# Second-layer trunk sums kept in PSUM over a chunk, four of its products by two levels, on one Trainium2 core

## The chip, the cores and the metric

The kernel runs on one core of a Trainium2 chip. The metric is the device time of one execution, in microseconds; lower is better. The engines are named as in the profile: TensorE (PE, with its weight loads as PEld) multiplies matrices, VectorE (DVE) and ScalarE (ACT) do elementwise work, GpSimd (POOL) does elementwise work and issues some DMAs, and SyncE (SP) issues most DMAs. SBUF is the on-chip memory, PSUM the eight accumulator banks that TensorE writes (each 128 partitions by 512 fp32 numbers).

## The reference

A retention block (a decayed linear attention) feeds a two-layer network with a leaky ReLU. Everything is fp32 in the result.

```python
# q, k, v: batch 4, 8 heads, 768 tokens, 64 dims
gamma = 1.0 - 2.0 ** (-5.0 - np.arange(H))
for t in range(S):
    state = gamma[None, :, None, None] * state + np.einsum('bhd,bhe->bhde', k[:, :, t], v[:, :, t])
    y[:, :, t] = scale * np.einsum('bhd,bhde->bhe', q[:, :, t], state)
x = y.transpose(0, 2, 1, 3).reshape(B * S, H * D)      # 3072 x 512
h = x @ w_in                                           # 512 -> 2048
g = np.maximum(0.01 * h, h)
return g @ w_out                                       # 2048 -> 512
```

## The kernel before

**Tiling.** The 768 tokens of each of the four sequences are cut into six chunks of 128, so a chunk c has 512 tokens in all. The 2048 hidden columns are cut into four units u of 512. For each pair (c, u) the kernel computes a hidden block (first layer), applies the leaky ReLU, and adds that unit's part to the output of the chunk (second layer). All matrix products of a pair are made by Strassen-Winograd: a 512x512x512 product is cut into 2x2 blocks of 256, and seven block products M1 to M7 replace eight. Their operands are blocks (b11, ...) and sums and differences of blocks, made on VectorE or GpSimd; their results are combined in PSUM and on VectorE.

**Two halves.** The first half (to about 285 us) covers chunks 0 and 1 and turns the weights from 64-bit to fp32. It also stores to DRAM the sums of first-layer weights ("kept") that the second half streams back. The second half runs over n = 0 to 15, n = 4(c-2) + u, in a loop at the end of the kernel. In this half the first layer is made by two levels of Strassen-Winograd: `inner_steps(n, group)` runs the second level for four of the seven products (group 0, weights `wa`, 28 matmuls of 128x128) or the other three (group 1, weights `wb`, 21 matmuls of 128x128), in banks 0 to 3, and `outer(n, group)` combines them on VectorE into g. The list INNER gives the order of the seven second-level products: M1, M5, M4, M6, M2, M3, M7. ScalarE copies M1's bank to the bank of M6 and M7, and takes four of the results out; VectorE adds the rest (L611 `plus`, L614 `minus`: nearly all VectorE additions have these two lines in the profile, so they are told apart by their tiles).

**The second layer.** For n = 0 to 3 and n = 15, `output` makes seven products of one level (28 matmuls of 128x256) in banks 5, 4, 7, 6 (called A, B, C, D), and each is added to the chunk's output tile o. For n = 4 to 14 (`by_leaves`), two ways are mixed. `trunk` makes four products by one level, M1 into A, M5 into C, M6 and M7 into B (16 matmuls of 128x256, L1299); A is copied to B after M1, B is added to o after M6 and again after M7, and `trunk_taken` adds A and C. The other three products (the "leaves") are made by the second level: `leaf_steps` (21 matmuls of 128x128, L1261, banks 6, 7, 2, 5), with weights that `sums_of_rows` made on VectorE in n = 0 to 3 and stored to DRAM (`leaf_kept`), and that `load_rows` reads back for every n. The moving operands are four differences on GpSimd (`leaf_sums`, L1252). The results stand in a tile and are added to o by an accumulating DMA issued from GpSimd (L1283), or on VectorE at the last unit of a chunk.

**Attention inside the loop.** While chunk c is in the network, the attention of chunk c+1 is made in pairs of sequences, at u = 0 and u = 1 (`visiting`, n = 0, 1, 4, 5, 8, 9). `joint_visit` makes the outputs of a pair in banks 1, 2, 0 and 7, and four VectorE instructions (L468) write them to x. `scores_of_pair` makes the scores (banks 0, 1) and state sums (banks 2, 3) of the pair that is visited next; VectorE masks the scores and adds the states. There are scores in n = 0, 1, 4, 5 and 8. `differences` and `sums_of_x` make the Strassen-Winograd operands of x.

**Order.** The order of the instructions on each engine is the order in which the program writes them; each engine runs its own queue in order. In a unit with leaves TensorE runs: first-layer group 0 of n+1; the visit; trunk M1, M5, M6; the scores; trunk M7; group 1 of n+1; the leaf. Where there are no scores, trunk M7 stands behind group 1. Units without a visit skip the attention parts. A DMA on SyncE's queue that waits holds up those behind it.

Of the kernel before, what the change touches and what calls it, by code (L numbers as in the profile page):

```python
# [18 lines left out]
C = 128  # L19
# [3 lines left out]
def kernel(  # L23
# [334 lines left out]
    def scores_of_pair(c, b, banks=None, mid=None):  # L358
# [28 lines left out]
        for j in range(2):  # L387
            am = work.tile([128, 2, HP // 2, 2, C // 2], FP32, tag=f"am{j}", name=f"am{j}_{c}_{b}")
            nc.vector.tensor_tensor(
                out=am.rearrange("p b m i t -> p (b m i) t"),  # L390
                in0=at[j].rearrange("p b m i t -> p (b m i) t"),
                in1=mask[:, 0].unsqueeze(1).to_broadcast([128, 2 * HP, C // 2]), op=ALU.mult)
            weights.append(am)
# [7 lines left out]
        if not last:  # L401
            state_of[p] = halves_of_states.pop(0)
            plus(state_of[p], mid, sums[1])
        mid_of[p] = old, mid
# [9 lines left out]
    def joint_visit(c, b, banks=None):  # L414

        later = following(c, b) if c > JOINED else None
        banks = banks or [[bank[k] for k in at] for at in ((1, 2), (0, 7))]
# [193 lines left out]
    def plus(out, a, b):  # L611
        nc.vector.tensor_tensor(out=out, in0=a, in1=b, op=ALU.add)  # L612

    def minus(out, a, b):  # L614
        nc.vector.tensor_tensor(out=out, in0=a, in1=b, op=ALU.subtract)  # L615
# [13 lines left out]
    def differences(x, t, last=True):  # L629

        minus(t[:, 0], x[:, 1], x[:, 0])
        minus(t[:, 1], x[:, 3], t[:, 0])
        minus(t[:, 2], x[:, 2], t[:, 1])
        if last:
            last_difference(x)

    def last_difference(x):
        minus(x[:, 1], x[:, 3], x[:, 1])
# [169 lines left out]
    last_three = {}  # L808
# [9 lines left out]
    def new_g(c, u):  # L818
        i = slot[0]
        slot[0] = 1 - i  # L820
        both = work.tile([128, 7, 2, N], FP32, tag=f"g{i}", name=f"g_{c}_{u}")
        last_three[c, u] = both[:, 2:5]
        return u, both[:, 0:4], Reversed(both)
# [309 lines left out]
    def sums_of_x(c, group):  # L1133
# [3 lines left out]
        for blocks, made in (((x[:, 0:1], made[:, :, 0:1]), (t, made[:, :, 1:4])) if group == 0 else  # L1137
# [5 lines left out]
            minus(b12, b22, b12)  # L1143
# [40 lines left out]
    leaf_kept = [dram.tile([128, 3, 7, C], FP32, name=f"leaf_kept_{u}") for u in range(NU)]  # L1184
# [3 lines left out]

    def leaf_rooms():

        free = [flat_of(unit(k)[:, 2:5]) for k in (1, 3, 5)]
        spare = [x2_place[0][:, 21 * C :], streamed_flat[0][:, 21 * C :]]
        more = [spare[i // 2][:, ds(i % 2 * 3 * C, 3 * C)] for i in range(4)]
        return free, spare, [x.rearrange("p (q n) -> p q n", q=3) for x in more]

    def rows_of(u):

        if u < NU - 1:
            return [((0, 3, 1), unit(2 * u + 1)[:, 2:5])]
        return [((0, 3, 2), units[2 * u + 1][1]), ((1, 2, 1), last_s4)]  # L1200

    def sums_of_rows(u):

        free, _, more = leaf_rooms()
        if u == NU - 1:
            more = more[0:2] + [x[:, 7 * C : 10 * C].rearrange("p (q n) -> p q n", q=3)
                                for x in free[0:2]]
        bases = []
        for at, blocks in rows_of(u):
            which = slice(*at)  # L1210
            a11, a21, a12, a22 = (blocks[:, :, k, ts(m, C)] for k in range(2) for m in range(2))
            r = [x[:, which] for x in more]
            plus(r[0], a21, a22)
            minus(r[1], r[0], a11)
            minus(r[2], a12, r[1])
            minus(r[3], a11, a21)
            bases.append((which, blocks))

        def keep():
            for which, blocks in bases:  # L1220
# [4 lines left out]
            for j, r in enumerate(more):  # L1225
                nc.sync.dma_start(out=leaf_kept[u][:, :, 3 + j], in_=r)
        return keep

    def load_rows(n):

        free, spare, _ = leaf_rooms()
        leaf_weights[:] = [x[:, 0 : 7 * C].rearrange("p (j n) -> p j n", j=7)
                           for x in (free[0], free[1], spare[1])]
        for to, kept_rows in zip(leaf_weights, (leaf_kept[at_of(n)[1]][:, i] for i in range(3))):
            nc.sync.dma_start(out=to, in_=kept_rows)

    leaf_weights = []

    def by_leaves(n):
        return n >= NU and n < N2 - 1  # L1240

    def leaf_sums(n):

        free, spare, _ = leaf_rooms()
        made = [x.rearrange("p (q n) -> p q n", q=3)
                for x in (free[0][:, 7 * C : 10 * C], free[1][:, 7 * C : 10 * C],
                          spare[0][:, 0 : 3 * C])]
        three = last_three[at_of(n)]
        b11, b12, b21, b22 = (three[:, :, k, ts(h, C)] for k in range(2) for h in range(2))
        for out, a, b in ((made[0], b12, b11), (made[1], b22, made[0]), (made[2], b21, made[1]),  # L1250
                          (b12, b22, b12)):
            nc.gpsimd.tensor_tensor(out=out, in0=a, in1=b, op=ALU.subtract)  # L1252
        return [b11, b21, *made, b22, b12]

    def leaf_steps(n, moving):

        ps = [bank[i][:, 0 : 3 * C].rearrange("p (i n) -> p i n", i=3) for i in (6, 7, 2, 5)]
        results = leaf_results()
        for m, q, j, s in INNER:
            for i in range(3):  # L1260
                nc.tensor.matmul(ps[q][:, i], lhsT=leaf_weights[i][:, j], rhs=moving[s][:, i],  # L1261
# [6 lines left out]
            elif m == "M7":  # L1268
                plus(results[:, :, 3], results[:, :, 3], ps[3])
                plus(results[:, :, 2], results[:, :, 2], ps[3])  # L1270
# [5 lines left out]
    def leaf_results():  # L1276
        return flat_of(unit(5)[:, 2:5]).rearrange("p (i q n) -> p i q n", i=3, q=4)

    def leaf_results_taken(c, o, final):

        results = leaf_results()
        if not final:
            nc.gpsimd.dma_start(out=o[:, 0:3].rearrange("p i k n -> p (i k n)"),  # L1283
                                in_=results.rearrange("p i q n -> p (i q n)"), accum_op=ALU.add)
            return
        for i in range(3):
            plus(o[:, i], o[:, i], results[:, i].rearrange("p (k h) n -> p k (h n)", k=2))
            nc.sync.dma_start(out=out[c, i], in_=o[:, i])

    def trunk(c, o, part, first, final):  # L1290

        u, g, gd = part
        ps = {x: room[x] for x in "ABC"}
        for m, x, sa, rhs, start in (("M1", "A", 0, g[:, 0], True), ("M5", "C", 4, gd[:, 0], True),
                                     ("M6", "B", 5, gd[:, 1], False),
                                     ("M7", "B", 1, g[:, 1], False)):
            for i in range(2):
                for k in range(2):
                    nc.tensor.matmul(ps[x][:, i, :], lhsT=block(2 * u + 1, sa)[:, k, ts(i, 128)],  # L1299
                                     rhs=rhs[:, k, :], start=(start and i == 0 and k == 0),  # L1300
                                     stop=(k == 1), skip_group_check=True)
            if m == "M1":
                nc.scalar.copy(out=ps["B"], in_=ps["A"])  # L1303
            elif m == "M6":
                if first:
                    nc.scalar.copy(out=o[:, 1], in_=ps["B"])
                else:
                    plus(o[:, 1], o[:, 1], ps["B"])
            elif m == "M7":
# [301 lines left out]
```

## Time and profile before

| | us |
|---|---|
| three runs | 634.63, 634.06, 633.66 (median 634.06) |
| the profiled execution, device time | 633.81 |
| its span in the profile | 632.1 |
| VectorE busy | 498.1 |
| ScalarE busy | 283.5 |
| GpSimd busy | 81.4 |
| DMA, mean over the span | 223 GB/s |
| granted TensorE clock | 1.00 |

A profile row reads: line, engine, operation, output tile <- input tiles, shape and count. One fp32 matmul of the program appears as two MATMUL records with two weight loads. In a timeline the first number is the start in microseconds from the start of the span and the second the time from the first start to the last end of the merged instructions; matmuls overlap their successors by some 0.16 us, so times between starts say what one costs. What stands in brackets is idle time and what ended it.

Start times of the units in the second half, taken from the first matmul of group 0 of n+1: n=1 before 285.9, n=2 at 304.98, n=3 at 328.01, n=4 at 351.04, n=5 at 378.02, n=6 at 405.08, n=7 at 427.62, n=8 at 450.16, n=9 at 477.16, n=10 at 502.88, n=11 at 525.42, n=12 at 547.97, n=13 at 570.84, n=14 at 593.38. The output of n=15 starts at 615.92, the last matmul at about 628.5.

### The profile page before, as it was taken

The page shows a single profiled execution, that of the slowest core. Times are in us where ns is not written, and L with a number is a line of the kernel's source. Part 1 is how long each engine was busy: PE and PEld are TensorE (multiplying, and loading weights), DVE is VectorE, ACT ScalarE, POOL GpSimd, SP SyncE. Part 2 cuts the span into 40 slices and gives each one's busy share as a digit, 9 for nine tenths or more (in the row PEclk, how much of TensorE's full clock was granted, in tenths as well). Part 3 has the DMA queues.
Part 4 walks back from the last instruction along what each step waited for, and adds up shares of the span by engine and source line. Part 5 has one row for each costly group of instructions (what it writes and reads, how often), then busy time and mean ns, then how long its engine had stood idle before and what let it go on. Part 6 is the DMA issues. An engine that isn't in the chain of part 4 may idle for free.

```text
span 632.1 us, 15063 instructions
## 1 busy us (share of the span) xinstructions
PE 624.7 (99%) x6284; PEld 570.5 (90%) x6284; DVE 498.1 (79%) x803; ACT 283.5 (45%) x559; POOL 81.4 (13%) x98
## 2 busy tenths in 40 slices
PE   8999999999999999999999999999999999999997
PEld 5888888888888889899999999999998999999996
DVE  5679769889979976668887768799848889866765
ACT  5876646347443114352442452634434424544540
POOL 2000000000011010101000033313033023033200
PEclk9999999999999999999999999999999999999999
DMA  8941325547772998295964888998479579689724
GB/s 330 404 138 34 133 67 208 163 145 226 260 276 81 334 350 289 89 347 168 340 209 157 280 293 250 342 293 260 157 240 306 159 230 278 206 263 271 192 45 116
DMA packets 103219, 141.18 MB, mean 223 GB/s; under 512 B 4328, under 2 KB 82024, under 8 KB 103152
## 3 DMA queue, kind: packets, MB, share of 16 engines
q1 hardware_dynamic: 101552, 132.53, 63.3%
q0 software_dynamic: 1296, 7.08, 5.6%
q8 instruction: 49, 0.80, 0.5%
q10 hardware_dynamic: 304, 0.62, 0.3%
q14 instruction: 18, 0.15, 0.1%
HBM read 108.49 MB, written 24.64 MB: 211 GB/s over the span
## 4 chain that ended last, share of the span: by engine, by line
PE 90%; DMA 5%; ACT 2%; DVE 2%; issue 0%; SPq 0%; DVEq 0%; ACTq 0%
PE bank L1348 26%; PE bank L1299 12%; PE bank L668 11%; PE bank L1261 8%; PE C_h L668 4%; PE B_o L668 4%; PE A_h L668 4%; PE A_o L668 4%; PE C_o L668 4%; PE B_h L668 4%; PE D_o L668 2%; PE D_h L668 2%; DMA x_words<-in_weights_dram 1%; DMA wa<-kept 1%; DMA in<-in_kv_dram 1%; PE bank L371 1%
## 5 line engine op out<-in xcount | busy, mean ns | idle before, releaser
L612 DVE TENSOR_TENSOR made<-made,bank 128x512 f32<-128x512 f32 (+1 forms) x96 | 56.1, 617 | 39.9 <-PE bank L1348 35.9
L1348 PEld LDWEIGHTS bank<-x,wb 128*128 128x128 f32 x672 | 77.6, 192 | 1.1 <-ACT bank L1352 0.3
L1348 PE MATMUL bank<-x,wb 128*128 128x128 f32 x672 | 77.9, 275 | 0.1
L612 DVE TENSOR_TENSOR o<-o,bank 128x512 f32<-128x512 f32 (+3 forms) x75 | 55.2, 767 | 24.3 <-ACT bank L782 6.2
L615 DVE TENSOR_TENSOR g<-g 128x512 f32<-128x512 f32 x96 | 64.1, 688 | 5.3 <-ACT g L1390 0.6
L1348 PE MATMUL bank<-x,wa 128*128 128x128 f32 x512 | 67.6, 275 | 0.0
L1299 PE MATMUL bank<-g,w 128*128 128x256 f32 x288 | 66.1, 382 | 0.7 <-DVE x L468 0.7
L1348 PEld LDWEIGHTS bank<-x,wa 128*128 128x128 f32 x512 | 62.8, 192 | 0.3
L1299 PEld LDWEIGHTS bank<-g,w 128*128 128x128 f32 x288 | 53.2, 190 | 8.0 <-DVE x L468 1.1
L1348 PE MATMUL bank<-t,wa 128*128 128x128 f32 x384 | 53.4, 275 | 0.1
L1348 PEld LDWEIGHTS bank<-t,wa 128*128 128x128 f32 x384 | 48.0, 192 | 0.3 <-DMA wa<-kept 0.3
L612 DVE TENSOR_TENSOR g<-made 128x512 f32<-128x512 f32 x64 | 44.0, 709 | 3.0
L1352 ACT COPY bank<-bank 128x512 f32<-128x512 f32 (+1 forms) x32 | 16.6, 520 | 60.1 <-PE bank L1348 59.8
L1390 ACT ACTIVATE g<-g 128x512 f32<-128x512 f32 x64 | 38.5, 631 | 8.2 <-DVE g L612 8.2
L668 PE MATMUL bank<-g,w 128*128 128x256 f32 x168 | 38.0, 382 | 0.0
L668 PEld LDWEIGHTS bank<-g,w 128*128 128x128 f32 x168 | 31.3, 190 | 4.2
L668 PE MATMUL bank<-g,last 128*128 128x256 f32 (+1 forms) x148 | 32.6, 375 | 0.0
L668 PEld LDWEIGHTS bank<-g,last 128*128 128x128 f32 x148 | 27.0, 190 | 3.9 <-DVE g L615 0.4
L1261 PE MATMUL bank<-g,w 128*128 128x128 f32 x176 | 26.8, 275 | 0.0
L668 PE MATMUL A_h<-x,w 128*128 128x256 f32 x112 | 26.6, 380 | 0.0
L1303 ACT COPY bank<-bank 128x512 f32<-128x512 f32 x11 | 6.3, 570 | 41.1 <-PE bank L1299 41.1
L1283 POOL DMA_DIRECT2D o<-w x9 | 8.1, 903 | 125.2 <-DVE g L615 65.6
(255 smaller groups left out, 1234.8 us busy)
## 6 DMA issues: line engine op xcount, KB each, us to landing
wa<-kept SPq DMA_DIRECT2D x16, 1344.0 KB, 9.4
raw<-in_weights_dram SPq DMA_DIRECT2D x31, 512.0 KB, 4.4
wb<-kept SPq DMA_DIRECT2D x16, 896.0 KB, 5.5
w<-leaf_kept SPq DMA_DIRECT2D x22, 448.0 KB, 4.6
wa<-kept SPq DMA_DIRECT2D x16, 448.0 KB, 6.1
wb<-kept SPq DMA_DIRECT2D x16, 448.0 KB, 6.3
o<-w POOLq DMA_DIRECT2D x9, 768.0 KB, 9.2
out_dram<-o SPq DMA_DIRECT2D x23, 256.0 KB, 2.5
```

The lines of the kernel that those rows point to most:

```text
L371: nc.tensor.matmul(at[j][ts(h, 64), n, m, i], lhsT=x[ts(j, 64), 1, a, ts(h, 64)], rhs=x[ts(j, 64), 0, a, ts(h, 64)], start=(n == 0 and a = ...
L612: nc.vector.tensor_tensor(out=out, in0=a, in1=b, op=ALU.add)
L615: nc.vector.tensor_tensor(out=out, in0=a, in1=b, op=ALU.subtract)
L668: nc.tensor.matmul(to, lhsT=block(w, sa)[:, k, ts(i, 128)], rhs=rhs[:, k, a:z], start=(first and (i == 0 or split) and n == 0 and k == 0), ...
L1261: nc.tensor.matmul(ps[q][:, i], lhsT=leaf_weights[i][:, j], rhs=moving[s][:, i], start=(i == 0 and m in ("M1", "M5", "M4")), stop=True, sk ...
L1283: nc.gpsimd.dma_start(out=o[:, 0:3].rearrange("p i k n -> p (i k n)"), in_=results.rearrange("p i q n -> p (i q n)"), accum_op=ALU.add)
L1299: nc.tensor.matmul(ps[x][:, i, :], lhsT=block(2 * u + 1, sa)[:, k, ts(i, 128)], rhs=rhs[:, k, :], start=(start and i == 0 and k == 0), sto ...
L1303: nc.scalar.copy(out=ps["B"], in_=ps["A"])
L1348: nc.tensor.matmul(ps[q][:, i], lhsT=w[:, j, i], rhs=part_of(moving[i], s), start=(i == 0 and m in ("M1", "M5", "M4")), stop=True, skip_gr ...
L1352: nc.scalar.copy(out=ps[3], in_=ps[0])
L1390: nc.scalar.activation(g[:, i], g[:, i], AF.Prelu, alpha=0.01)
```

## The change

- **Trunk.** It keeps three products only: M1 in A (bank 5), M5 in C (bank 7), M6 in B (bank 4), 12 matmuls of 128x256. The three banks are not taken out after each unit; they accumulate over all leaf units of a chunk. At the last leaf unit of the chunk `trunk_taken` copies A out, forms a, ab = a+B and abc = ab+C in three blocks of the leaf's result tile, and adds them to o: o0 at once, the rest in a second part that stands after group 1 of n+1.
- **Leaves.** M7 joins the products by two levels, so there are four: 28 matmuls of 128x128. Banks are 0, 2, 1, 6, and the order is M1, M5, M2, M6, M4, M3, M7. Leaf sums on GpSimd are 512 wide. The last result block is added to another, and the whole 128x2048 result is added to o by one VectorE instruction at the next unit's start (at a new chunk: after `outer` of group 0, with the stores of the finished chunk behind it); at u = 0 the results are written straight into o.
- **Units.** n=3 becomes a leaf unit too, with weights that are still on the chip. `sums_of_rows` makes four rows instead of three, for two of the four units on GpSimd.
- **Weights in halves.** Four rows are loaded instead of three; at u = 0 of a chunk the first two are loaded at the end of the unit before, the other two after the visit's v load.
- **Attention.** Visits of later chunks use bank 6 in place of 7. In leaf units the scores use banks 1 and 6, and the second mask comes after the state sums. `outer` of group 0 stands after the visit. GpSimd's leaf sums wait for VectorE's last difference or sum of x, where there are no scores to make.

```diff
+        masks(range(1 if second_mask_last else 2))
...
+        if second_mask_last:
+            masks((1,))
...
-        banks = banks or [[bank[k] for k in at] for at in ((1, 2), (0, 7))]
+        banks = banks or [[bank[k] for k in at] for at in ((1, 2), (0, 7 if c == JOINED + 1 else 6))]
...
+    ON_CHIP = {NU - 2: 1, NU - 1: 3}
+    FIRST_LEAVES = NU - 1
...
+    def by_leaves(n):
+        return FIRST_LEAVES <= n < N2 - 1
...
+    def load_rows(n, rows=range(4)):
+
+        free = leaf_rooms()
+        if rows[0] == 0:
+            leaf_weights.clear()
+        for i in rows:
+            to = free[(1, 3)[i // 2]][:, ds(i % 2 * 7 * C, 7 * C)]
+            to = to.rearrange("p (j n) -> p j n", j=7)
+            nc.sync.dma_start(out=to, in_=leaf_kept[at_of(n)[1]][:, i])
+            leaf_weights.append([to[:, j] for j in range(7)])
...
     def leaf_steps(n, moving):
 
-        ps = [bank[i][:, 0 : 3 * C].rearrange("p (i n) -> p i n", i=3) for i in (6, 7, 2, 5)]
-        results = leaf_results()
-        for m, q, j, s in INNER:
-            for i in range(3):
-                nc.tensor.matmul(ps[q][:, i], lhsT=leaf_weights[i][:, j], rhs=moving[s][:, i],
+        ps = [bank[i].rearrange("p (i n) -> p i n", i=4) for i in (0, 2, 1, 6)]
+        results = leaf_results(n)
+        leaf_weights[:] = of_unit.pop(n, leaf_weights)
+        for m, q, j, s in LEAVES:
+            for i, to in enumerate(TARGETS):
+                nc.tensor.matmul(ps[q][:, to], lhsT=leaf_weights[i][j], rhs=moving[s][:, i],
...
+        plus(results[:, :, 2], results[:, :, 2], ps[3])
+        plus(results[:, 2], results[:, 2], results[:, 3])
+        if at_of(n)[1] > 0:
+            unadded.append(lambda: plus(flat_of(os[at_of(n)[0]]), flat_of(os[at_of(n)[0]]),
+                                        results.rearrange("p i q n -> p (i q n)")))
...
+    def trunk(n, part):
 
         u, g, gd = part
-        ps = {x: room[x] for x in "ABC"}
-        for m, x, sa, rhs, start in (("M1", "A", 0, g[:, 0], True), ("M5", "C", 4, gd[:, 0], True),
-                                     ("M6", "B", 5, gd[:, 1], False),
-                                     ("M7", "B", 1, g[:, 1], False)):
+        first = n == FIRST_LEAVES or u == 0
+        for x, sa, rhs in (("A", 0, g[:, 0]), ("C", 4, gd[:, 0]), ("B", 5, gd[:, 1])):
...
+    def trunk_taken(n, o):
+
+        a, ab, abc = (flat_of_k(leaf_results(n)[:, i]) for i in range(3))
+        nc.scalar.copy(out=a, in_=room["A"])
+        plus(o[:, 0], o[:, 0], room["A"])
+        plus(ab, a, room["B"])
+        plus(abc, ab, room["C"])
+
+        def rest():
+            plus(o[:, 2], o[:, 2], ab)
+            plus(o[:, 1:4:2], o[:, 1:4:2], abc.unsqueeze(1).to_broadcast([128, 2, 2, N]))
+        return rest
...
+    LEAVES = [INNER[i] for i in (0, 1, 4, 3, 2, 5, 6)]
...
+        if u > 0:
+            add_results()
...
+        if visiting:
+            if u == 0:
+                xs[c + 1] = new_x(c + 1)
+            joint_visit(c + 1, 2 * u)
+            if leaves:
+                load_rows(n, range(4)[2 if u == 0 else 0 :])
+        elif leaves and u == NU - 1:
+            behind = sums_of_x(c + 1, 1)
+        if more:
             outer(n + 1, 0)
+        if leaves and u == 0:
+            finish_chunk(c - 1)
+            os[c] = new_o(c)
+        if visiting and u == 1:
+            behind = differences(*xs[c + 1])
+        elif c + 1 < NC and u == 2:
+            behind = sums_of_x(c + 1, 0)
+        if leaves:
+            moving = leaf_sums(n, behind if not scores_next else None)
+            trunk(n, part)
+            if visiting and not scores_next:
+                fill(6, 2, start=False)
...
+        if last_leaves:
+            rest = trunk_taken(n, os[c])
+            if n + 2 == N2:
+                rest()
+        if scores_next and leaves:
+            scores_of_pair(*scores_next, [bank[i] for i in (1, 6, 2, 3)], second_mask_last=True)
...
+        if n in (0, 1):
+            keep.append(sums_of_rows(n))
+        if n in (1, 2):
+            keep.append(sums_of_rows(n + 1, nc.gpsimd))
         if more:
             inner(n + 1, 1)
+            if last_leaves and n + 2 < N2:
+                rest()
...
+            leaf = leaf_steps(n, moving)
+            last_one = n + 2 == N2
+            for count, ready in ((1, 1), (1, 1), (2, 2)) if last_one else (
+                    (4, 2 if u == NU - 1 else 3), (1, 2 if u == NU - 1 else 1)):
+                products(leaf, count)
+                for _ in range(ready):
+                    later.pop(0)()
```

`finish_chunk(c)` adds what is unadded and stores the four blocks of o; `add_results` runs the pending 128x2048 addition. `later` holds the leaky ReLUs of g on ScalarE, which are put between leaf copies.

## The prediction

> **What bounds the kernel now.** I read the totals first, then TensorE's order of time, then the places where it halts. Times below are starts in the profiled execution (span 632.1 us, device time 633.81 us; the median of the three runs, 634.06 us, lies 0.25 us above it).
>
> ```profile
> span 632.1 us, 15063 instructions
> PE 624.7 (99%) x6284; PEld 570.5 (90%) x6284; DVE 498.1 (79%) x803; ACT 283.5 (45%) x559; POOL 81.4 (13%) x98
> ```
>
> TensorE is busy for 99%, so an edit is worth what it takes from TensorE's own stream, or from TensorE's halts; work on VectorE (79%) counts only where TensorE waits for it. TensorE's timeline of one unit without attention (n=6) gives the prices:
>
> ```profile
> 410.67 0.83 PE L1348 MATMUL bank<-t,wa 128*128 128x128 f32 x6
> 411.34 5.34 PE L1299 MATMUL bank<-g,w 128*128 128x256 f32 x24
> 416.52 4.85 PE L1348 MATMUL bank<-x,wb 128*128 128x128 f32 x42
> 421.21 1.89 PE L1299 MATMUL bank<-g,w 128*128 128x256 f32 x8
> 422.94 0.61 PE L1261 MATMUL bank<-g,w 128*128 128x128 f32 x4
> ...
> 427.40 0.39 PE L1261 MATMUL bank<-g,wb 128*128 128x128 f32 x2
> ```
>
> One fp32 matmul of the program is two records. The start-to-start distances: 24 wide records take 416.52-411.34 = 5.18 us, so a 128x256 matmul costs 0.432 us; 42 narrow ones take 4.69 us, so a 128x128 matmul costs 0.223 us. There is no hole: the end of one group is the start of the next.
>
> Where TensorE does halt in the second half I find three places. In the chain of waits around 485 us (n=9):
>
> ```profile
> 485.00 1.44 DVE made L612
> ...
> 486.53 1.30 DVE g L612
> 487.83 0.34 DVE x L468
> 488.18 0.04 issue
> 488.22 3.72 PE bank L1299 x16
> ```
>
> The trunk's second product goes into bank 7, which the attention visit left full; its evacuation (L468) stands behind two VectorE additions that took 1.44 and 1.30 us instead of the usual 0.69, because GpSimd was making the leaf sums. The 24 trunk records last 6.25 us (485.53 to 491.78) against 5.38 in the same place at n=4 (359.41 to 364.79): 0.87 us lost. At n=12 the 42 records from 559.40 last 5.03 us instead of 4.69: 0.34 lost, because ScalarE's copy that they need stands behind copies of the output:
>
> ```profile
> 560.13 0.59 ACT L1324 COPY o<-bank 128x512 f32<-128x512 f32 x1
> 560.60 0.60 ACT L1325 COPY o<-bank 128x512 f32<-128x512 f32 x1
> 561.08 0.51 ACT L1352 COPY bank<-bank 128x384 f32<-128x384 f32 x1
> ```
>
> At the last unit a weight load waits for VectorE's difference of g (PEld, 0.39 us at 617.80); by record distances about 0.25 is lost.
>
> **TensorE's own work.** Counting both built programs: 128x128 matmuls go from 1023 to 1128, 128x256 from 764 to 704, and one bf16 fill is added. Of the 12 two-level units, 11 (n=4..14) had 16 wide + 21 narrow and get 12 wide + 28 narrow; n=3 goes from 28 wide to that. So 105 x 0.223 - 60 x 0.432 = 23.4 - 25.9 = **-2.5 us**. The fill (256 columns) is at most half of a 512-column bf16 fill of the first half of this trace (0.216 us): +0.1. Together -2.4.
>
> Here a rule speaks against the change. The Trainium skill ("TensorE: Matmul & The Clock Gate", Back-to-back issue gap) says that in a stream of weight load and matmul pairs both set the spacing, with 81 ns at 128 columns and 131 ns at 512. Interpolated that is 98 ns at 256, and a narrow matmul would cost 0.83 of a wide one, 0.36 us on this kernel's scale; the exchange would then add 105 x 0.36 - 25.9 = +12 us (estimate). The rows say 0.223/0.432 = 0.52, in both widths with a fresh weight load for each matmul. I take the rows: these very operands run beside each other.
>
> **Halts that go.** n=9: visits of later chunks use bank 6 instead of 7, the outer additions come after the visit's evacuation, and GpSimd's leaf sums wait for VectorE's last input difference ("behind"): -0.87. One re-entry after the halt costs 0.10 more (a normal wide record starts 0.216 us after the last, here one came 0.32 after): -0.1. n=12: sums A, B, C stay in banks 5, 4, 7 over the chunk, so those o copies go: -0.34. Last unit: with 6.2 us of leaf instead of 4.7, the g differences, which stand ahead of the leaf evacuations in VectorE's order, end before their product: -0.25. Sum **-1.6**. What is late next at n=9 is nothing near: bank 7 has no visitor.
>
> **VectorE, ScalarE, GpSimd.** Per unit, trunk additions of about 3.6 us (0.6+1.2+0.6+1.2, at 421 to 426 and before) go; come: leaf additions one block wider and one more 128x512 (+1.0), and one 128x2048 addition (2.3 us, about four times the 0.6 us step of the 128x512 `o<-o,w` additions at n=12). That is even, and lies under TensorE's 22.5 us. Of GpSimd, nine accumulating DMA issues (0.9 us each) go; each leaf sum grows from 384 to 512 columns: between 1.04 us (a 512-column decay beside an idle VectorE) and 1.33 (in proportion to the 1.00 us of 384). I take 1.3, so four end 5.3 us after their start; at n=6 that is about 2 us before the leaf product that needs each. New at n=1, 2 are 16 GpSimd operations for weight rows; VectorE has idle stretches there (1.2 us before 299.40, 1.3 before 302.33), and their reader is the leaf of n=3: hidden.
>
> **Waits that come.** (a) Scores to second inner group, n=4, 5, 8. Before, the trunk's fourth product (1.83 us) lay between them; it goes. Banks 1, 2, 3 hold scores and state sums, and the group writes them 0.7, 1.3 and 2.0 us after the scores' end. At n=4 VectorE has: mask (0.65), state (0.65), state (0.65, after the former), then ScalarE's copy into bank 3 (0.5). The mask starts 1.0 us early, as the order puts it first; the two states end about 1.5 after the scores, the copy 2.1: 0.15 late. At n=5 and 8 there is one state sum: no halt, if VectorE is free when the scores come. Before it stand the x evacuation, outer, and the 128x2048 sum (n=4, 8) or four input differences (n=5): free about 1 us early, or about when needed if GpSimd's decays get in between. Bounds for the three: 0 to 1.5; I take 0.15.
> (b) Chunk ends n=3, 7, 11. The sums in banks go through three blocks of the leaf's result room (ab, abc), read by the second part of the sums after the second inner group; the leaf's first result copy on ScalarE must wait for it, the later copies queue behind, and leaf products M3 and M7 need them. By VectorE's order at n=7 this part ends 3.0 us after the inner group if no addition waits for GpSimd, 4.1 if each waits for one leaf sum. M3 stands if the copy has not landed 4.4 us after the inner group; the copy takes 0.65. So 0 to 0.6 us per end, 0.3 taken at n=7 and n=11; n=3 has no 128x2048 sum at its start and none. Sum 0.6.
>
> That such alternation is real shows at n=7 now, where VectorE's sums of x (0.55 us alone) stand among GpSimd's:
>
> ```profile
> 431.56 1.36 DVE L615 TENSOR_TENSOR x<-x 128x384 f32<-128x384 f32 x1
> 432.95 2.50 DVE L615 TENSOR_TENSOR x<-x,x 128x384 f32<-128x384 f32 x2
> 435.38 1.35 DVE L615 TENSOR_TENSOR x<-x 128x384 f32<-128x384 f32 x1
> ```
>
> There the change starts GpSimd after these four: they shrink to 2.3 us in all, but the next two meet it.
>
> **DMA.** Four rows of 448 KB per unit replace three and the 768 KB accumulation. Without a visit they are issued at the leaf's end, 16 us before use; three land in 4.6 to 6 us now. At n=5 they queue on SP behind the v load, about 9 us into the unit; the third was issued at 388.5 and landed within 6.3 us, by 394.8, a fourth by about 397, and the leaf starts at about 398.6 (378.0 + 6.4 + 2.0 + 5.4 + 2.0 + 4.8): hidden by 1.5 us. Output stores wait on SP for the 128x2048 sum; behind them stand the k and wa loads, which must wait for the scores' end anyway. The row stores at n=0..3 grow by a third, under 16 us of slack: nothing. o has one buffer, so the leaf's copies at n=8 and 12 wait for the stores: at n=12 they land about when the first copy is due, 2 us before a product needs it.
>
> **Sum:** -2.4 - 1.6 + 0.15 + 0.6 = -3.2 us: 633.81 becomes 630.6, and the median, 0.25 above, **630.9 us** (-0.5%). The first 285 us and the tail after the last matmul have the same instructions.
>
> **Rivals.**
> 1. Halts only move (20%): the exchange holds but hand-overs (a), (b) take their upper bounds, 1.5 + 1.2: 634.06 - 4.0 + 2.7 = **632.8 us**, down to 632. For it: VectorE is 79% busy and loses its cover at three places. Against: the halts of now cost only 1.5 us in 280.
> 2. Slower (8%): at the hand-over from scores to inner group VectorE is not an instant late but a whole queue: two or three of its two-SBUF-input operations each wait 1.0 to 1.4 us for a decay or leaf sum, and so do the chunk ends. It decides from 0.9 us at each of the six places (6 x 0.9 = 5.3 over the 4.0 + 1.3); at 1.1 each the time is 634.06 - 4.0 + 6.6 = **636.7 us**. Against: masks and state sums read PSUM, and such additions kept 0.68 us beside GpSimd at 394.19.
> 3. It doesn't act (7%): rows arrive late at n=5, or the narrow leaf, four weights a product, is not at 0.223: the gain is lost, **634 us**.
>
> **Numbers.** The main case (65%) is 629.7 to 632. A difference under 0.2% (1.3 us) can't be told from none by this measurement. Faster by more (below 632.8): 0.65 + 0.17 = 0.82; same: 0.11; slower 0.07. The range, 629.6 (all halts gone, nothing new, and 0.5 for the runs' spread) to 633.0, leaves out rival 2, part of rival 3 and a little below.
>
> **What would show it.** In the new profile: trunk groups of 24 wide records at 5.2 us and leaf groups of 56 narrow ones at 6.2, back to back; a no-visit unit of 22.4 instead of 22.5 us, n=3 of about 22.4 instead of 23.0; the 488 us halt gone; holes under 0.2 us behind the scores, under 0.6 in the leaf at n=7 and 11. Wrong if the narrow matmuls spread, or if a hole over 1 us stands before the second inner group or in a leaf.

## The result and the profile after

| | before | after |
|---|---|---|
| median of 5 runs each, us | 633.91 (633.24 to 634.63) | 631.10 (630.24 to 631.22) |
| ratio, 95% interval | | 0.9952 [0.9937, 0.9966] |
| span of the profiled execution, us | 632.1 | 629.3 |
| start of n=2, us | 304.98 | 305.50 |
| start of n=2 to the last matmul, us | 323.23 | 320.03 |

The forecast was 630.9 us. The totals of the changed kernel:

```profile
span 629.3 us, 15220 instructions
PE 622.8 (99%) x6375; PEld 572.2 (91%) x6375; DVE 512.4 (81%) x793; ACT 281.4 (45%) x543; POOL 105.8 (17%) x109
```

TensorE is the bound as before; VectorE has 14 us more work, GpSimd 24 us more, and neither decides. TensorE's timeline of the unit without attention (n=6; start, length, engine, operation, count):

```profile
411.21 5.35 PE L1351 MATMUL bank<-g,w 128*128 128x256 f32 x24
416.39 4.85 PE L1390 MATMUL bank<-x,wb 128*128 128x128 f32 x42
421.08 1.06 PE L1311 MATMUL bank<-g,w 128*128 128x128 f32 x8
421.98 1.06 PE L1311 MATMUL bank<-x,w 128*128 128x128 f32 x8
422.87 1.09 PE L1311 MATMUL bank<-g,w 128*128 128x128 f32 x8
423.79 1.06 PE L1311 MATMUL bank<-wb,w 128*128 128x128 f32 x8
...
427.37 0.28 PE L1390 MATMUL bank<-x,wa 128*128 128x128 f32 x1
```

The trunk is 24 wide records in 416.39 - 411.21 = 5.18 us, the leaf 56 narrow ones in 427.37 - 421.08 = 6.29. In the leaf, one product takes 0.89 or 0.90 us, but M2 (from 422.87) 0.92: its first matmul comes 0.03 us late. It writes the bank of M1, which ScalarE copies from just before. The halt of n=9 is gone from the chain of waits (start, length, what):

```profile
484.69 0.47 PE bank L453 x32
485.15 5.38 PE bank L1351 x24
490.53 0.11 PE bank L707
490.64 0.45 PE bank L1390 x4
```

The 24 trunk records follow the visit and last 5.38 us instead of 6.25; the row of L707 is the added fill, 0.11 us. The length of every unit, from its first matmul of group 0 to the next unit's:

| unit | before | after | difference |
|---|---|---|---|
| n=1 | 27.50 | 27.70 | +0.20 |
| n=2 | 23.03 | 23.03 | 0 |
| n=3 | 23.03 | 22.41 | -0.62 |
| n=4 | 26.98 | 27.15 | +0.17 |
| n=5 | 27.06 | 26.84 | -0.22 |
| n=6, 7, 10, 11, 13, 14, each | 22.54 | 22.41 to 22.44 | -0.13 (n=6: -0.10) |
| n=8 | 27.00 | 26.94 | -0.06 |
| n=9 | 25.73 | 24.74 | -0.99 |
| n=12 | 22.88 | 22.41 | -0.47 |
| output of n=15 to the last matmul | 12.29 | 12.03 | -0.26 |

Together -3.0 us. The profiled execution after also came to n=1 0.3 us later than the one before (277.80 against 277.49), although both have the same instructions up to 257 us, so its span is only 2.8 us shorter.

### The profile page after: what moved, and what is told of

It reads as the page before. It is cut to its first block, busy times and chain, and to the rows that moved or that the text cites. A ratio compares the mean times of both kernels' runs of the same rounds, so it can differ in the third digit from the quotient of the medians.

```text
span 629.3 us, 15220 instructions
## 1 busy us (share of the span) xinstructions
PE 622.8 (99%) x6375; PEld 572.2 (91%) x6375; DVE 512.4 (81%) x793; ACT 281.4 (45%) x543; POOL 105.8 (17%) x109
## 4 chain that ended last, share of the span: by engine, by line
PE 94%; DVE 2%; ACT 1%; DMA 1%; issue 0%; SPq 0%; DVEq 0%; ACTq 0%
PE bank L1390 27%; PE bank L1311 12%; PE bank L1351 10%; PE bank L674 9%; PE C_h L674 4%; PE B_o L674 4%; PE A_h L674 4%; PE A_o L674 4%; PE C_o L674 4%; PE B_h L674 4%; PE D_o L674 2%; PE D_h L674 2%; PE d L695 2%; DMA raw<-in_weights_dram 1%; PE bank L371 1%; PE bank L453 1%
## 5 line engine op out<-in xcount | busy, mean ns | idle before, releaser
L619 DVE TENSOR_TENSOR g<-made 128x512 f32<-128x512 f32 x64 | 49.0, 786 | 2.9
L1351 PE MATMUL bank<-g,w 128*128 128x256 f32 x216 | 48.5, 381 | 0.0
L1311 PE MATMUL bank<-g,w 128*128 128x128 f32 x368 | 47.0, 276 | 0.0
L1351 PEld LDWEIGHTS bank<-g,w 128*128 128x128 f32 x216 | 40.3, 190 | 5.4
L1311 PEld LDWEIGHTS bank<-g,w 128*128 128x128 f32 x368 | 43.8, 192 | 0.0
L1290 POOL TENSOR_TENSOR x<-g 128x512 f32<-128x512 f32 x12 | 16.6, 1382 | 138.2 <-DVE t L622 40.1
L674 PE MATMUL bank<-g,w 128*128 128x256 f32 x168 | 38.0, 382 | 0.0
L674 PEld LDWEIGHTS bank<-g,w 128*128 128x128 f32 x168 | 31.3, 190 | 4.2
L619 DVE TENSOR_TENSOR o<-o,bank 128x512 f32<-128x512 f32 (+2 forms) x44 | 26.5, 633 | 9.8 <-ACT bank L788 4.2
L619 DVE TENSOR_TENSOR o<-o,w 128x2048 f32<-128x2048 f32 (+2 forms) x17 | 28.9, 1722 | 0.2
L163 POOL TENSOR_TENSOR in<-in,dec 128x512 f32<-128x512 f32 x2 | 2.4, 1232 | 139.7 <-DMA in<-in_kv_dram 139.7
```

Of the source, the lines that this page charges most:

```text
L619: return nc.vector.tensor_tensor(out=out, in0=a, in1=b, op=ALU.add)
L674: nc.tensor.matmul(to, lhsT=block(w, sa)[:, k, ts(i, 128)], rhs=rhs[:, k, a:z], start=(first and (i == 0 or split) and n == 0 and k == 0), ...
L1290: op = nc.gpsimd.tensor_tensor(out=out, in0=a, in1=b, op=ALU.subtract)
L1311: nc.tensor.matmul(ps[q][:, to], lhsT=leaf_weights[i][j], rhs=moving[s][:, i], start=(i == 0 and m in ("M1", "M5", "M4")), stop=True, skip ...
L1351: nc.tensor.matmul(room[x][:, i, :], lhsT=block(2 * u + 1, sa)[:, k, ts(i, 128)], rhs=rhs[:, k, :], start=(first and i == 0 and k == 0), s ...
```

## The experiments

The theory under test is the prediction's sum: a narrow matmul costs 0.22 us however many stand in a leaf, three halts go, and small hand-overs come. Its rivals are that narrow matmuls spread, that the gain came from the halts alone, and that one of the accompanying edits (order, masks, two-part chunk ends, halved loads) is what holds the time. Each run alters the changed kernel unless another is named. A time without an interval is that of one execution, its profiled one.

**What a narrow matmul costs.** Each leaf product issues its fourth block's matmul a second time, so 84 narrow matmuls are added, and the second-layer results count that block twice.

```diff
+            nc.tensor.matmul(ps[q][:, to], lhsT=leaf_weights[i][j], rhs=moving[s][:, i],
+                             start=False, stop=True, skip_group_check=True)
             if m == "M1":
```

> The kernel after, with every narrow matmul of the fourth leaf block (M7's) issued twice, so that its sums are not the reference's. That is 7 more 128x128 matmuls in each of 12 units, 84 in all, with no new evacuation. If a narrow matmul costs what the rows of before show, 0.223 us, the time grows by 18.7 us, to about 649.8, and a leaf lasts 7.8 us instead of 6.2. Rival, the width rule of the Trainium skill on this kernel's scale (0.36 us each): 30 us more, 661. Rival that TensorE is not the bound in leaf units: less than 10 us more.

Measured: 649.66 us, (649.66 - 631.10)/84 = 0.221 us each, against 0.223 by the prediction's rows. TensorE's timeline of its n=6 (L1314 is the added one):

```profile
425.70 1.06 PE L1311 MATMUL bank<-g,w 128*128 128x128 f32 x8
426.59 0.39 PE L1314 MATMUL bank<-g,w 128*128 128x128 f32 x2
426.82 1.06 PE L1311 MATMUL bank<-x,w 128*128 128x128 f32 x8
```

The added matmul takes 426.82 - 426.59 = 0.23 us, in a stream in which every matmul has a fresh weight load. Five in a row per product do not spread, and the ratio of 0.83 to a wide matmul, which the prediction had interpolated, does not hold for this fp32 stream.

**n=3 by one level again.** This undoes the leaf at n=3 alone.

```diff
-    FIRST_LEAVES = NU - 1
+    FIRST_LEAVES = NU
...
-        elif leaves and u == NU - 1:
+        elif more and u == NU - 1:
...
-            finish_chunk(c - 1)
+            if c > 3:
+                finish_chunk(c - 1)
```

> The kernel after, with n=3 made in one level as before (28 wide matmuls, the chunk's output finished there), all later units as after. This undoes the exchange in one unit alone. By the prices of the rows: 16 more wide, 28 fewer narrow, 6.91 - 6.24 = 0.66 us more in that unit, a length of 23.0 instead of 22.4 us, and 631.7 us. Rival, that the gain comes from what VectorE and ScalarE no longer take out: the unit's length stays within 0.2 us of after. Rival, that the narrow leaf is dearer in place than by its rows: the unit becomes shorter.

Measured: 632.20 us. n=3 is 23.03 us, 0.62 longer, so the exchange has the predicted size there. Another 1.25 us came at a place that was not expected: n=4 lasts 28.40 us instead of 27.15. (The whole execution is only 1.10 us longer because it came to n=2 0.79 us earlier.) Timeline of that place; in brackets the idle time before and its releaser:

```profile
365.19 2.04 POOL L163 TENSOR_TENSOR v<-v,dec 128x512 f32<-128x512 f32 x2 [6.65 <-DMA v<-in_kv_dram]
...
366.28 0.56 PEld L382 LDWEIGHTS bank<-v,k 64*64 64x64 f32 x32 [0.74 <-POOL v L163]
```

TensorE waits for v, which GpSimd decays when the load has landed; in the changed kernel the same GpSimd work began at 363.23. v was issued at the same time in both (359.27 and 359.44), but here three output stores of chunk 2 had held the first two weight rows on SyncE's queue from 354.06 to 356.66, just ahead of v. That these rows delay v is read from the queue and was not tried by itself. It is no gain over the kernel before, where n=4 lasts 26.98 us: it shows that weight rows loaded early and output stores of the finished chunk get in each other's way on one queue.

**The halts alone.** The kernel before, without its halts at n=9 and n=12: GpSimd's leaf sums wait for the last input difference, and the last chunk's two output copies go from ScalarE to VectorE.

```diff
+            op = nc.gpsimd.tensor_tensor(out=out, in0=a, in1=b, op=ALU.subtract)
+            if behind is not None:
+                tc.add_manual_dep(op.ins, behind.ins.name, IN_ORDER, reason="one port for both")
+                behind = None
...
-        if first:
+        if first and c == NC - 1:
+            nc.vector.tensor_copy(out=o[:, 0], in_=room["A"])
+            nc.vector.tensor_copy(out=o[:, 3], in_=room["C"])
+            plus(o[:, 1], o[:, 1], room["C"])
+        elif first:
```

> The kernel before, with two of its three halts taken away and nothing else of the change: GpSimd's leaf sums wait for VectorE's last difference or sum of x where there are no scores to make, and at n=12 two of the three output copies go from ScalarE to VectorE. My theory: 0.97 us at n=9 and 0.34 at n=12 go, so 1.3 us less than before (ratio 0.998, about 632.6 beside 633.9), with no change of a TensorE instruction. Rival, that the halts are made up for later or move to another wait: no difference.

Measured: 632.26 us (632.09 to 632.92) against 633.59 for the kernel before, 0.9981 [0.9972, 0.9989]. n=9 falls from 25.73 to 24.76 and n=12 from 22.88 to 22.54: 1.31 us. (n=4 is 0.14 longer in its profile, all of it in TensorE's state sums, 1.18 us instead of 1.04.) So nearly half of the change's gain can be had with two small edits and the old arithmetic; the rest needs the exchange.

**The second mask in its old place.**

```diff
-            scores_of_pair(*scores_next, [bank[i] for i in (1, 6, 2, 3)], second_mask_last=True)
+            scores_of_pair(*scores_next, [bank[i] for i in (1, 6, 2, 3)])
```

> The kernel after, with both masks before the state sums again, in the banks of after. Theory: at n=4 the two states end 0.6 us later, so TensorE's hole in the inner group grows from 0.2 to 0.8 us; at n=5 and n=8 the one state sum ends 0.6 later and makes a hole of 0.1 to 0.2: 0.8 to 1.0 us in all, about 632. Rival, that the hand-over has slack: no new hole, 631.1.

Measured: 631.68 us, but n=4 is only 27.31 (+0.16) and n=5 +0.06; n=8 is unchanged. The rest (n=6 22.72, a late weight load that this edit does not touch) is not the mask's. The expectation was four times too large. The timeline at n=4 shows why; first the changed kernel, then this one:

```profile
365.90 0.69 DVE L392 TENSOR_TENSOR am<-bank,mask 128x512 f32<-128x512 f32 x1 [1.67 <-PE bank L371]
...
366.93 0.69 DVE L619 TENSOR_TENSOR half_states<-states,bank 128x512 f32<-128x512 f32 x1 [0.34 <-PE bank L382]
367.72 0.69 DVE L619 TENSOR_TENSOR more_states<-half_states,bank 128x512 f32<-128x512 f32 x1
...
368.50 0.46 ACT L1394 COPY bank<-bank 128x384 f32<-128x384 f32 x1 [12.31 <-PE bank L1390]
```

```profile
365.84 1.29 DVE L392 TENSOR_TENSOR am<-bank,mask 128x512 f32<-128x512 f32 x2 [1.67 <-PE bank L371]
...
367.05 0.68 DVE L619 TENSOR_TENSOR half_states<-states,bank 128x512 f32<-128x512 f32 x1
```

VectorE stands idle for 0.34 us before the first state sum, since TensorE has not finished it. With one mask the sum starts 1.03 us after the first mask (366.93 - 365.90), with two 1.21 (367.05 - 365.84): the second mask costs 0.18 us and not its own 0.60. A step that fills a wait costs what sticks out.

**Chunk ends in one part.**

```diff
-            if n + 2 == N2:
-                rest()
+            rest()
...
-            if last_leaves and n + 2 < N2:
-                rest()
```

> The kernel after, with the chunk ends in one part: the sums ab and abc are added to o at once, ahead of the second inner group's evacuations in VectorE's order. Theory: at n=7 and n=11 these two additions (0.7 and 1.2 us, two SBUF inputs) meet GpSimd's last two leaf sums and put off VectorE by 2 to 3 us, so that the leaf's product M4 finds bank 1 full and the next unit's group finds its banks late: 0.5 to 1.0 us more at each of n=7 and n=11, less at n=3, 1 to 2 us in all, about 632.5. Rival, that it is all hidden under TensorE: 631.1 and units of 22.4 us.

Measured: 631.60 us. n=3, 7 and 11 keep 22.41 us, so at its own place the one-part end is hidden. But n=8, the unit after, is 27.36 instead of 26.94. Two places of its timeline:

```profile
442.58 3.41 DVE L619 TENSOR_TENSOR o<-o,w 128x512 f32<-128x512 f32 x2
...
443.20 1.71 POOL L1290 TENSOR_TENSOR g<-g 128x512 f32<-128x512 f32 x1
...
456.68 0.56 PEld L436 LDWEIGHTS bank<-qk,states 64*64 64x64 f32 x32 [0.33 <-DVE made L619]
```

The two output sums (the second one wide) take 3.41 us beside GpSimd's leaf sums, where the two-part end took 1.82 after the inner group. VectorE then works without a break from there to 456 us, and hands the delay on: the visit of n=8 needs a bank that VectorE empties late. The price of a delay on VectorE is paid where its queue next meets TensorE, 14 us later. The other lengthened unit (n=5, +0.30) has a weight load that waits 0.22 us for the load of `wa`; whether the edit brings that about is not shown.

**The leaf in another order.** M4 before M2 and M6, to take the 0.03 us at M2 away.

```diff
-    LEAVES = [INNER[i] for i in (0, 1, 4, 3, 2, 5, 6)]
+    LEAVES = [INNER[i] for i in (0, 1, 2, 4, 3, 5, 6)]
```

> The kernel after, with M4 between M5 and M2 in the leaf. In after every leaf has a hole of 0.03 us at M2's first matmul. Theory: M2 adds to M1's bank and has to wait until ScalarE has copied M1 out, with one product in between; with two the holes go, 0.03 x 12 = 0.36 us. At n=6 and n=10 M4 then needs GpSimd's third sum 1.8 us after the leaf's start, and in after it ends 1.81 and 1.84 after it: new holes of 0.1 to 0.2 there. Sum 0 to -0.2 us; a free leaf of 6.25 us instead of 6.29. Rival, that the hole comes from the weights or the moving tile: it stays.

Measured: 646.66 us, 15.6 us longer, 14.5 of them between the start of n=2 and the last matmul: a miss. The 0.03 us went, but every unit with a leaf became 0.9 to 1.4 us longer. Timeline of the leaf of n=6:

```profile
429.97 1.67 ACT L1432 ACTIVATE g<-g 128x512 f32<-128x512 f32 x3
430.07 0.97 PEld L1311 LDWEIGHTS bank<-g,w 128*128 128x128 f32 x8
...
431.54 0.57 ACT L1321 COPY w<-bank 128x512 f32<-128x512 f32 x1
...
432.26 0.46 PE L1311 MATMUL bank<-g,w 128*128 128x128 f32 x2 [1.02 <-ACT w L1321]
```

M7 adds to the bank of M6, so M6's result must be copied out first. The program puts three leaky ReLUs on ScalarE after the fourth leaf step. In the kept order M6 is the fourth step and its copy stands ahead of them; here it is the fifth, behind 1.67 us of activations.

**The same order, with the leakies one step later.**

```diff
-            for count, ready in ((1, 1), (1, 1), (2, 2)) if last_one else (
-                    (4, 2 if u == NU - 1 else 3), (1, 2 if u == NU - 1 else 1)):
+            for count, ready in ((1, 1), (1, 1), (3, 2)) if last_one else (
+                    (5, 2 if u == NU - 1 else 3), (1, 2 if u == NU - 1 else 1)):
```

> The leaf's order of the run before (M4 before M2 and M6), but with the ScalarE leaky ReLUs of the next unit put behind the fifth leaf step in place of the fourth, so that the copy of M6's bank stands ahead of them again. My theory: the 1.18 us hole before M7 in each leaf came from the leakies standing ahead of M6's copy on ScalarE; it goes, the 0.03 us at M2's first matmul stays away (12 times, -0.36), and M4 waits some 0.1 us for its room at n=6 and n=10 (+0.2): 631.0, all units within 0.1 of the changed kernel's. Rival (the hole comes from M7 standing too close behind M6 whatever ScalarE's queue holds): about 1 us a leaf stays, 643 to 646 us.

Measured: 633.44 us. The large hole is gone, so ScalarE's order was its cause. The timeline of ScalarE at the end of n=7:

```profile
447.46 2.26 ACT L1321 COPY w<-bank 128x512 f32<-128x512 f32 x4 [1.38 <-DVE o L619]
...
449.62 1.67 ACT L1432 ACTIVATE g<-g 128x512 f32<-128x512 f32 x3
```

All four copies, M6's among them, now stand ahead of the leakies. But units without a visit are 22.54, 0.13 longer than the changed kernel's: M7's first two matmuls lose 0.09 and 0.07 us, since only M3 (0.89 us) now stands between M6 and M7, and the 0.03 at M2 is saved. n=6 and n=10 lose 0.29 more waiting for GpSimd's third leaf sum, which M4 reads. So the rival held in the small: closeness costs 0.16 a leaf. The kept order, M2 and M6 before M4, is worth some 2 us over this one.

**GpSimd's leaf sums without the wait.**

```diff
-            moving = leaf_sums(n, behind if not scores_next else None)
+            moving = leaf_sums(n)
```

> The kernel after, with GpSimd's leaf sums no longer waiting for VectorE's last difference or sum of x. Theory: at n=9 the visit's evacuation is late again, but nobody waits for bank 6, so no hole comes back there; at n=3, 7 and 11 the four sums of x are spread to 1.3 us each, VectorE comes to the chunk end some 3 us later, and the leaf's first copy waits: 0.5 to 1.5 us more at each of n=7 and n=11, 1 to 3 in all, 632 to 634. Rival, that the wait mended n=9: 0.9 us at n=9 and nothing elsewhere.

Measured: 632.34 us. n=9 keeps 24.74: the wait is not what removed that halt here. n=7 and n=11 become 23.34 and 23.35, +0.93 each. Timeline of n=7, first the changed kernel, then this one:

```profile
436.34 0.55 DVE L622 TENSOR_TENSOR x<-x 128x384 f32<-128x384 f32 x1
436.93 1.15 DVE L622 TENSOR_TENSOR x<-x,x 128x384 f32<-128x384 f32 x2
...
438.71 1.56 POOL L1290 TENSOR_TENSOR x<-g 128x512 f32<-128x512 f32 x1 [14.15 <-DVE x L622]
```

```profile
435.35 1.26 POOL L1290 TENSOR_TENSOR wb<-g,x 128x512 f32<-128x512 f32 x1
435.54 1.49 DVE L622 TENSOR_TENSOR x<-x 128x384 f32<-128x384 f32 x1
436.70 1.47 POOL L1290 TENSOR_TENSOR more_room<-g,wb 128x512 f32<-128x512 f32 x1
437.07 3.05 DVE L622 TENSOR_TENSOR x<-x,x 128x384 f32<-128x384 f32 x2
...
440.17 1.05 PE L1390 MATMUL bank<-x,wb 128*128 128x128 f32 x7 [0.67 <-DVE x L622]
```

Beside GpSimd three of the sums of x take 1.5 us each instead of 0.55, and the second inner group, whose operands they are, waits. The wait was expected to matter in the leaf; it matters in the inner group. The Trainium skill ("SBUF — State Buffer", Who interferes with whom) says that a VectorE instruction with two SBUF inputs contends with a GpSimd instruction that reads SBUF; the trace agrees, 0.55 against 1.5.

**The outer additions ahead of the visit.** In all six units with a visit, `outer` of group 0 goes back to its place in the kernel before.

```diff
         if visiting:
+            outer(n + 1, 0)
...
-        if more:
+        if more and not visiting:
             outer(n + 1, 0)
```

It came from a hole of the changed kernel at n=1 that the prediction did not have. Timeline of the changed kernel (L163 is GpSimd's decay of v, L1249 its first sum for the new weight rows):

```profile
291.11 1.49 POOL L163 TENSOR_TENSOR v<-v,dec 128x512 f32<-128x512 f32 x1
291.62 1.53 DVE L622 TENSOR_TENSOR x<-x 128x512 f32<-128x512 f32 x1
...
292.56 1.72 POOL L1249 TENSOR_TENSOR w<-w 128x512 f32<-128x512 f32 x1
...
294.27 1.27 DVE L392 TENSOR_TENSOR am<-bank,mask 128x512 f32<-128x512 f32 x2
...
295.47 0.67 DVE L619 TENSOR_TENSOR more_states<-half_states,bank 128x512 f32<-128x512 f32 x1
...
296.25 0.69 DVE L619 TENSOR_TENSOR states<-more_states,bank 128x512 f32<-128x512 f32 x1
...
297.02 0.46 ACT L1394 COPY bank<-bank 128x384 f32<-128x384 f32 x1 [7.06 <-DVE states L619]
...
297.53 0.86 PEld L1390 LDWEIGHTS bank<-x,wb 128*128 128x128 f32 x7 [0.15 <-ACT bank L1394]
```

ScalarE's copy goes into a bank that VectorE's state sum empties at 296.94. The last two input differences ahead of it took 1.5 us each beside the decays of v; in the kernel before only the last one did.

> The kernel after, with the outer additions ahead of the visit's evacuation again, in units with a visit. Theory: at n=1 VectorE did them while it waited for the visit; behind it they put the input differences later, two of which then meet GpSimd's decays (1.5 us instead of 0.7), and the state sums come late: the hole of 0.23 us at n=1 goes, nothing else changes, 630.9. Rival, that the hole at n=1 comes from GpSimd's new weight row sums: it stays.

Measured: 630.10 us; n=1 27.50, n=4 27.04, n=8 26.84. The hole at n=1 is gone with the weight row sums still in place, so the rival is out. The next two expectations are for six runs of this kernel and of the changed one on one chip; the edit is the same as above, and "row sums" in the first should read "visit's evacuation":

> The changed kernel with the first of the next unit's outer additions put ahead of the row sums at n=1 and n=4 (the run with one look gave 630.1), now timed. Theory: the two holes of 0.23 and 0.20 us go, and nothing else moves: 0.4 us under the changed kernel on the same chip, a ratio to the kernel before of about 0.9945. Rival (the single look was a lucky one): no difference between the two, 0.995.

> The changed kernel as it is, timed beside the run above on the same chip, as its yardstick: 631.1 us, a ratio of 0.9952 to the kernel before, some 0.4 us above the run above by the theory, level with it by the rival.

Measured: 630.48 us (630.09 to 631.49), 0.9942 [0.9921, 0.9963]; the changed kernel 630.73 us (630.59 to 630.97), 0.9944 [0.9925, 0.9962]. These do not tell the two apart. The profiles do by a little: n=1 is 27.65 against 27.81, n=4 27.05 against 27.15 and n=8 26.84 against 26.94, but n=5 26.93 against 26.84. At n=4 it is TensorE's state sums that got shorter (1.04 us against 1.15); the 0.20 us hole in the inner group stayed, against the expectation. At n=1 the changed kernel lost its time elsewhere in this execution, in TensorE's state sums, which waited for v:

```profile
292.78 0.56 PEld L382 LDWEIGHTS bank<-v,k 64*64 64x64 f32 x32 [0.24 <-POOL v L163]
```

With `outer` ahead, n=1 too kept 0.15 us of that wait in this execution. By unit lengths the edit may be worth 0.2 to 0.3 us; the times do not confirm it, and no more is claimed.

**The weights not in halves.** All four rows of a chunk's first unit are loaded after the visit.

```diff
-                load_rows(n, range(4)[2 if u == 0 else 0 :])
+                load_rows(n)
...
-            elif u == NU - 1:
-                load_rows(n + 1, range(2))
```

> The four leaf weight rows of a chunk's first unit are all loaded behind the visit, in place of two at the end of the unit before and two behind the visit: two more transfers of about 0.46 MB each stand late, and none early. My theory: the leaf of that unit starts some 13 us behind the visit, a row landed in some 4 us in the trace of the changed kernel, so four rows that queue up still arrive in time and the halves are worth nothing: units 4, 8 and 12 keep their lengths (27.15, 26.94, 22.41 us) within 0.1, the run stays at 631.1 +- 0.5. Rival (the halves are what keeps the leaf fed): the first leaf group of n=4 and n=8 waits for its weights, 0.5 to 2 us each, 632 to 635 us.

Measured: 631.85 us. n=4, n=8 and n=12 keep 27.15, 26.94 and 22.41: no leaf waits for its rows, and the halves show no gain there. The longer time is n=5 (+0.22) and n=9 (25.63, +0.89). At n=5 a weight load waits 0.14 us for the load of `wa`, which stands behind these rows on SyncE's queue; but two runs that leave the halves have such a wait too (0.22 and 0.24 us), so it is not shown to be the edit's. Chain of waits of n=9:

```profile
484.87 0.84 PE bank L1351 x3
485.71 0.62 issue
486.34 4.80 PE bank L1351 x21
```

"issue" means that the profile shows nothing that TensorE waited for. A 16 KB packet of the instruction queue was in flight at 483.92 to 485.02, later in the unit than in the changed kernel (482.51 to 483.74). That TensorE lacked instructions would fit, but in the run with n=3 by one level such a packet came later still (487.02 to 488.00, 9.2 us into the unit instead of 7.5) and nothing was lost. It was not tested; the cause is open, and so is whether this edit brings it about.

## Why the prediction was right, point by point

- **Exchange, -2.4: direction and price right, 0.37 us too large.** A narrow matmul costs 0.22 us (0.221 in the doubled leaf), a wide one 0.43; n=3 gave 0.62 of its 0.67. A unit without attention should have gained 16 x 0.432 + 21 x 0.223 - 12 x 0.432 - 28 x 0.223 = 0.167 us and gained 0.13. What the term lacked is the 0.03 us at M2 in each of 12 leaves. The fill cost 0.11, predicted 0.1.
- **Rule against row:** the ratio of 0.83, an estimate interpolated from two figures of the Trainium skill ("TensorE: Matmul & The Clock Gate", Back-to-back issue gap), would have made the change 12 us slower. The row's 0.52 was right.
- **Halts, -1.6: right in size and place.** n=9 -0.99, with the unit's exchange, the fill and M2 taken out -0.96 (predicted -0.97); n=12 -0.33 (-0.34); the last unit -0.26 (-0.25). The run of the kernel before without the first two gained 1.3. Of the three cures named for n=9, the wait of GpSimd is not needed in the changed kernel, but in the kernel before it was enough by itself. The later outer additions are not needed either: with `outer` ahead, n=9 keeps 24.74. The other bank was not tried by itself.
- **VectorE, GpSimd, ScalarE hidden: right but for n=1.** The 128x2048 sum took 2.29 us (2.3 predicted), a leaf sum 1.27 (1.3). GpSimd's weight row sums are hidden, as predicted: at n=1 the first begins at 292.56, when the decays of v are done, and the hole there goes without them being touched. What failed at n=1 is a step that the prediction put at nothing: `outer` behind the visit, which it counted as a cure at n=9 and at no cost elsewhere. It also took the first 285 us as unchanged, but VectorE's order differs from n=0 on (258 us). At n=1 the four input differences begin 10.94 us into the unit instead of 10.62, and so meet GpSimd's two decays of v otherwise. In ten profiled executions with the changed program at n=1, six have two differences of 1.5 us instead of one, and a hole of 0.1 to 0.25 us in the inner group as above; in the other four the second decay begins 0.3 us later, and TensorE's state sums wait for v by as much. The unit lasts 27.60 to 27.81, on average 27.72, against 27.50 before: +0.22.
- **New wait (a), 0.15: right.** 0.20 at n=4 by ScalarE's copy, which starts at 368.50, and none at n=5 and 8.
- **New wait (b), 0.6: did not come.** The lower case held. The timeline of n=7:

```profile
444.63 1.82 DVE L619 TENSOR_TENSOR o<-o,w 128x512 f32<-128x512 f32 x2
...
446.54 1.56 ACT L1321 COPY w<-bank 128x512 f32<-128x512 f32 x3 [1.38 <-DVE o L619]
```

The second part ends 446.45 - 443.49 = 2.96 us after the inner group (predicted 3.0 in this case), as GpSimd's last leaf sum is through at 444.55, before it starts; ScalarE's copies follow at once, and the leaf has no hole. The middle of the bounds was taken where the end without contention was true.

- **DMA hidden: right.** At n=5 the four rows, issued from 386.99, landed in a median of 7.4 us, ahead of the leaf at 398.6.

Put together: -2.0 (exchange, with M2 and fill) - 1.6 + 0.2 + 0 + 0.2 = -3.2, measured -3.0 over the units. What is left lies in TensorE's state sums: 1.14 us instead of 1.04 at n=4, 1.13 instead of 1.04 at n=8, 1.04 instead of 1.12 at n=5. The prediction had no term for it. Both runs with `outer` ahead have 1.04, 1.12 and 1.04 again, so this too comes with `outer` behind the visit; how is not shown. The forecast met 631.10 within 0.2 by luck in part: two errors of opposite sign (0.6 of chunk ends too many, 0.6 at n=1 and M2 too few) cancelled. Of the rivals, "halts only move" was the nearest: 0.8 us of small hand-overs came, a third of its price.

## What to carry to other kernels

Where TensorE is busy for 99%, price an exchange by start-to-start distances of the very shapes in the stream, and then look for the new writer of each bank: what must have been copied out, and which queue that copy stands in. A step moved on an in-order engine is judged by what stands behind it: three activations ahead of one copy cost 14.5 us over twelve leaves here, while a mask in front of a state sum cost under 0.2, since it filled a wait. A delay that shows nothing in its own unit can be paid in the next, so compare all unit lengths, not the one edited. And a cure for one unit acts in all that share the code: `outer` behind the visit, which n=9 did not need with the other cures in place, cost 0.2 to 0.3 us at n=1, 4 and 8 by their lengths, after the small gain at n=5.

## What was not expected of the hardware

- Up to 257 us all fourteen profiled kernels have the same instructions, and yet n=0 begins between 248.80 and 250.56 us in them. This spread is a good part of the difference between single executions, and unit lengths, which repeat to 0.01 us where nothing halts, tell more than times.
- TensorE can lose 0.9 us with nothing in the profile to wait for (n=9 without the halves, 25.63 instead of 24.74), and a late weight load lengthens one unit by 0.2 to 0.3 us in some executions (n=5, n=6) and not in others.
